# A planned attention and feed-forward kernel: a later due time for the codes of item 23, and pair 19 turned by TensorE

## The chip, the cores and the metric

The kernel runs on one core of one Trainium2 chip. The metric is the device time of one execution in microseconds; the time of a kernel is the median of its runs.

## The reference

There are two stages. In the first, 4 batches of 8 heads with 768 tokens and 64 features attend within clusters: a query sees only the keys that have the same nearest of 16 centroids.

```python
q_assign = np.argmax(np.einsum('bhsd,hcd->bhsc', q_n, c_n), axis=-1)
k_assign = np.argmax(np.einsum('bhsd,hcd->bhsc', k_n, c_n), axis=-1)
mask = q_assign[:, :, :, None] == k_assign[:, :, None, :]
scores = scale * np.matmul(q, k.transpose(0, 1, 3, 2))
scores = np.where(mask, scores, -1000000000.0)
...
attn = np.exp(scores)
attn = attn / (np.sum(attn, axis=-1, keepdims=True) + 1e-09)
return np.matmul(attn, v).astype(np.float32)
```

In the second, the heads of a token are put side by side to a row `x` of 512 values, and 3072 such rows go through a feed-forward layer with 2048 hidden values:

```python
h = x @ w_in
g = h * (1.0 / (1.0 + np.exp(-h)))
return (g @ w_out).astype(np.float32)
```

## The kernel before, in words

**The work.** An *item* `h8` to `h31` is one head of batches 1 to 3, its queries and keys (batch 0 is written out by hand as `plan`). An item's rows are loaded (`load`, line 111), split into two half-precision parts on VectorE (`hi`, line 127, and `lo`, line 132) and turned by a transposing transfer on SP's queue into the tile `ab` (`xpose`, line 141). Then TensorE makes the logits against the centroids (`logits_1`, line 180, 12 small matmuls into `psN`); VectorE sums them, finds the largest and marks it (lines 192, 208, 217). The marks are the item's *codes*: GpSimd scales them (lines 224 and 225), SP turns them (`c_xpose`, line 233, tile `cdt`), and GpSimd's queue moves them into 16 further rows of `ab` (`c_move`, line 237). From then on one matmul over `ab` gives the scores with the mask in them.

**Score units.** There are 192; each is two matmuls of line 356 (`qk_mm`, into one of two `pS` buffers) and one exponential on ScalarE (line 361). Item 23, the last head of batch 2's first half to be reached, is first read by unit 117. When the six units of a pair of heads and one half of the queries are through, 36 matmuls of line 373 (`pv`) multiply with the values, and VectorE normalizes (lines 383 and 385) to the tile `xn`, 128 by 384 values.

**Turned pairs.** Such a *pair* has a number n: n // 8 is the batch, n // 4 % 2 the half of the queries, n % 4 the pair of heads. It must be turned into a quarter of `xt`, the input of the up projection: either by a transposing transfer on SP's queue (`xn_d`, line 414), or by three transposes on TensorE into a PSUM bank `px` (`xn_t`, line 395) and a copy by VectorE or ScalarE (`xn_ev`, lines 406 and 404). `by_dma(n)` chooses.

**Feed-forward.** An up projection (`unit_a`, line 423) is four matmuls, one for each quarter of `xt`, into `ph`; ScalarE and VectorE gate it. The down projections are groups of four matmuls (line 494) or products of eight with sums ahead of them (line 576).

**Order.** There is one queue for each engine and each waits in order. From unit 27 on the order is set by a planner, when the kernel is built: it keeps a clock for each engine, knows for each piece a ready time, a length and a rank, and takes on TensorE what is ready at its clock, the lowest rank first; the other engines take what is ready first. For a score unit the ready time holds `code_at` of its items, which is the planned landing of the codes and a margin (`CODES`, 1.5, for the items of batches 2 and 3). PSUM banks 0 to 3 go around in the order in which the planner has them free. A piece that the planner puts first is waited for on the chip, whether or not something behind it could run.

Of the kernel before, what the change touches and what calls it, by code (L numbers as in the profile page):

```python
# [34 lines left out]
def kernel(  # L35
# [11 lines left out]
    B, H, S, D = q.shape  # L47
# [68 lines left out]
    def hi(job, eng=None, part=None):  # L116
        s = part or slice(0, job.n)
        if job.name not in hls:
            n = len(hls)
            hls[job.name] = mp.tile([128, 12, 2, D], f16, name="hl", tag=f"hl{n % 4 if n < EARLY else n % 3}", bufs=1)  # L120
        o, i = hls[job.name][:, s, 0, :], raws[job.name][:, s, :]
        if eng == "act":
            nc.scalar.activation(out=o, in_=i, func=AF.Copy, bias=0.0, scale=QS)  # L123
        elif eng == "pool":
            nc.gpsimd.tensor_scalar(out=o, in0=i, scalar1=QS, scalar2=None, op0=ALU.mult)
        else:
            nc.vector.tensor_scalar(out=o, in0=i, scalar1=QS, scalar2=None, op0=ALU.mult)

    def lo(job, part=None):
        s = part or slice(0, job.n)  # L130
        hl = hls[job.name]
        nc.vector.scalar_tensor_tensor(  # L132
            out=hl[:, s, 1, :], in0=raws[job.name][:, s, :], scalar=QS, in1=hl[:, s, 0, :], op0=ALU.mult, op1=ALU.subtract
        )

    def xpose(job, part=None):
        s = part or slice(0, job.n)
        hl = hls[job.name]
        if job.name not in abs_:
            abs_[job.name] = mp.tile([128, 12, 128], f16, name="ab", tag=f"ab{place[job.name] % 12}", bufs=1)  # L140
        nc.sync.dma_start_transpose(abs_[job.name][:, s, :], hl[:, s].rearrange("p n c d -> p (n c d)"))
# [44 lines left out]
    def logits_1(job):  # L186
        logits_n(job, None, 2 * HC)

    def lsum(job, last=True):
        g, m, P = job.halves, job.m, Ls[job.name]  # L190
        L = mp.tile([128, 12 * HC], f32, name="L", bufs=2)[:, 0 : g * HC * m].rearrange("p (h c m) -> p h c m", h=g, m=m)
        nc.vector.tensor_reduce(  # L192
            out=L, in_=P.rearrange("p h (n c) m -> p h c m n", n=2), axis=AX.X, op=ALU.add
        )
        if last:
            done(psNs.pop(job.name))
        Ls[job.name] = L
# [7 lines left out]
    def mx_n(job):  # L205
        g, m = job.halves, job.m
        mx = mxn[job.name] = mp.tile([128, 12], f32, name="mxn", bufs=3)
        nc.vector.tensor_reduce(
            out=mx[:, 0 : g * m].rearrange("p (h m) -> p h m", h=g), in_=Ls[job.name].rearrange("p h c m -> p h m c"),
            axis=AX.X, op=ALU.max,  # L210
        )

    def ge_n(job):
        g, m = job.halves, job.m
        nn[job.name] = len(nn)
        mx = mxn.pop(job.name)[:, 0 : g * m].rearrange("p (h m) -> p h m", h=g)
        nc.vector.tensor_tensor(  # L217
            out=ohv(job), in0=Ls.pop(job.name), in1=mx.unsqueeze(2).to_broadcast([128, g, HC, m]), op=ALU.is_ge
        )


    def c_scale(job):
        o = ohv(job)
        nc.gpsimd.tensor_scalar(out=o[:, :, :, 0:3], in0=o[:, :, :, 0:3], scalar1=OHV, scalar2=None, op0=ALU.mult)  # L224
        nc.gpsimd.tensor_scalar(
            out=o[:, :, :, 3:6], in0=o[:, :, :, 3:6], scalar1=OHV, scalar2=-OHV, op0=ALU.mult, op1=ALU.add
        )
# [3 lines left out]
    def c_xpose(job):  # L231
        cd = cds[job.name] = mp.tile([128, 2, 128], f16, name="cdt", tag="cd", bufs=4)
        nc.sync.dma_start_transpose(cd, ohd[nn[job.name] % 3].rearrange("p h n -> p (h n)"))

    def c_move(job):
        cd = cds.pop(job.name)
        nc.gpsimd.dma_start(
            abs_[job.name][64 : 64 + HC, :, :].rearrange("p n c -> p (n c)"), cd[0 : 6 * HC].rearrange("p h c -> p (h c)")
        )

    def cd_mm(job):
        m = (job.n + 1) // 2
        if job.name not in psNs:
            psNs[job.name] = bank("psC")
        for h in range(2):
            nc.tensor.matmul(
                psNs[job.name][0 : m * HC, 256 + 128 * h : 384 + 128 * h], ohv(job)[:, h].rearrange("p c m -> p (c m)"), ident, start=True, stop=True
            )
# [730 lines left out]
    def lands(t, work, rest):  # L979
        nonlocal moves_end  # L980
        moves_end = max(t, moves_end) + work
        return moves_end + rest

    def add(eng, ready, length, f, then=None, late=0.0):
        lanes[eng].append((ready, ready + late, length, f, then))
# [17 lines left out]
    def either(ready, dve, act, f, then=None, late=0.0):  # L1003
        eng = "ACT" if backlog("ACT", ready) + act + MARGIN < backlog("DVE", ready) + dve else "DVE"
        add(eng, ready, act if eng == "ACT" else dve, lambda: f(eng[0]), then, late)
# [6 lines left out]
    code_at, tensor_todo, after_unit, turn_at, after_turn = {}, [], {}, {}, {}  # L1012

    def chain(job, b):
        def split(t):
            old = int(job.name[1:]) - (3 if int(job.name[1:]) >= H + 8 else 4)
            if old >= H + 2 and old not in turn_at:
                after_turn[old] = split
                return
            if job.name not in loaded:  # L1020
                waiting[job.name] = split
                return
            t = max(t, loaded[job.name] + 0.4, turn_at.get(old, 0.0) + 0.3)
            either(t, 0.5, 0.72, lambda e: hi(job, "act" if e == "A" else None), lambda t: add("DVE", t, 0.9, lambda: lo(job), turned, 1.5), 1.5)

        def turned(t):
            i = int(job.name[1:])
            split_at.setdefault(i, t)
            if i in after_split:
                after_split.pop(i)(t)  # L1030
            u = last_use.get(place[job.name] - 12, 0)
            if u not in read_at:
                after_unit.setdefault(u, []).append(lambda x: turned(max(t, x)))
                return
            t = max(t, read_at[u] + 0.06)
            add("SP", t, lambda t: min(max(1.7, moves_end - t), 8.0), lambda: xpose(job), lambda t: landed(lands(t, 1.49, 1.41)), 0.0 if b == 1 else 3.0)

        def landed(t):
            i = int(job.name[1:])
            turn_at[i] = t  # L1040
            t_start(t)
            if i in after_turn:
                after_turn.pop(i)(t)
            turning(t + ROOM[b - 1])

        def turning(t):
            tensor_todo.append((t, 0.35, lambda: logits_1(job), sums))

        def sums(t):
            add("DVE", t + 0.2, 0.52, lambda: lsum(job), lambda t: add("DVE", t, 0.47, lambda: mx_n(job), top, 0.6), 0.6)  # L1050

        def top(t):
            add("DVE", t, 0.33, lambda: ge_n(job), codes, 0.6)

        def codes(t):
            if job.late:
                add("POOL", t, 1.05, lambda: c_scale(job), lambda t: add("SP", t, 1.3, lambda: c_xpose(job), moved))
            else:
                tensor_todo.append((t + 0.06, 0.11, lambda: cd_mm(job), out_of_bank))

        def moved(t):
            add("POOL", lands(t, 0.71, 1.4) + 0.1, 0.58, lambda: c_move(job), lambda t: known(t, 0.52, 0.87, CODES))

        def out_of_bank(t):
            either(t + 0.2, 0.44, 0.44, lambda e: cd_ev(job, e), lambda t: by_sync(t), 0.3)

        def by_sync(t):
            clock["SP"] = max(clock["SP"], t) + 0.65
            known(clock["SP"], 0.63, 0.98, 1.0)

        def known(t, work, rest, room):
            code_at[job.name] = lands(t, work, rest) + room

        return split

# [63 lines left out]
    for i in range(H, B * H):  # L1139
        b, h = divmod(i, H)  # L1140
        p = SPLIT[i - H]
        job = jobs[i]
# [58 lines left out]
    def t_start(t):  # L1201
        ready_t[0] += 1
        if ready_t[0] == B * H - H + 1 and any(n > 1 for x in QUADS.values() for n in x):
            t_step(0, t, 1)
# [20 lines left out]
    work = {hb: 16 * 0.655 + sum(3.452 if x in (0, 1, 2) else 6.118 for x in kinds[hb]) for hb in kinds}  # L1225
# [2 lines left out]
    unit = FIRST  # L1228

    def by_dma(n):  # L1230
        return 8 <= n < 8 * B - 1 and n != 11

    def norm_piece(n, t):
        b, c, i = n // 8, n // 4 % 2, n // 8 * H + 2 * (n % 4)
# [381 lines left out]
    while True:  # L1616
# [11 lines left out]
        t, e, piece = best  # L1628
# [34 lines left out]
```

## Time and profile before

| what | us |
|---|---|
| median of 3 runs (lowest, highest) | 298.42 (297.69, 299.86) |
| the profiled execution | 297.59 |
| its span, first to last instruction | 295.8 |
| busy: TensorE, VectorE, ScalarE, GpSimd | 286.2, 234.8, 228.5, 72.0 |

The profile is of one execution, 0.83 us under the median of the three runs. PE is TensorE's matmuls, PEld its weight loads, DVE VectorE, ACT ScalarE, POOL GpSimd, SP the queue that issues most transfers; a q behind an engine's name is its queue of instructions that only issue. A row's L number is a line of the kernel.

### The profile page before, as it was taken

Reading aid. Unit: us, or ns where it says so; the run is one execution under the profiler, and the core shown is the slowest. Engines: PE = TensorE matmul, PEld = TensorE weight load, DVE = VectorE, ACT = ScalarE, POOL = GpSimd, SP = SyncE. Lnnn points to the kernel's source line nnn. Section 1 sums busy time; section 2 is a strip of 40 time slices with the busy share of each in tenths; the row PEclk is TensorE's granted clock in tenths of the full one; section 3 lists DMA queues with packets and bytes.
Section 4 is the critical chain, followed back from the end, with each engine's and each line's share of the span. In section 5 each row is a group of like instructions: output and inputs, shape, how many; then the busy total and the mean of one; then the engine's idle time right before and its main releaser. Section 6 shows DMA issues by size and latency. Waiting matters only on the chain.

```text
span 295.8 us, 8471 instructions
## 1 busy us (share of the span) xinstructions
PE 286.2 (97%) x3369; PEld 209.2 (71%) x3369; DVE 234.8 (79%) x517; ACT 228.5 (77%) x385; POOL 72.0 (24%) x130
## 2 busy tenths in 40 slices
PE   7999989999999999999999899999999999999995
PEld 3777746566766566668766775768787878888984
DVE  5999688486897799997797845989868788778862
ACT  5999789755996579988588577997889987967621
POOL 5485610001041015653232471224210000000000
PEclk9999999999999999999999999999999999999999
DMA  6869999998966499999947969896130011110013
GB/s 208 268 170 198 231 217 194 120 296 175 252 147 166 123 193 271 226 192 228 215 137 149 199 165 259 185 150 133 32 99 17 13 51 51 49 39 2 11 63 142
DMA packets 78710, 44.63 MB, mean 151 GB/s; under 512 B 56240, under 2 KB 75600, under 8 KB 78672
## 3 DMA queue, kind: packets, MB, share of 16 engines
q1 hardware_dynamic: 71840, 35.50, 53.7%
q0 software_dynamic: 6288, 8.13, 14.3%
q8 instruction: 26, 0.43, 0.6%
q10 hardware_dynamic: 544, 0.48, 0.5%
q14 instruction: 12, 0.10, 0.1%
HBM read 27.30 MB, written 6.29 MB: 114 GB/s over the span
## 4 chain that ended last, share of the span: by engine, by line
PE 80%; DMA 13%; ACT 3%; issue 1%; DVE 1%; SPq 0%; POOL 0%; ACTq 0%; DVEq 0%
PE ph L423 19%; PE pS L356 17%; PE po L576 15%; PE pO L373 9%; PE po L494 8%; PE ph L717 5%; DMA win_s<-in_moe_w_in_dram 4%; PE psN L180 3%; DMA ab<-hl 2%; DMA vn<-in_v_dram 2%; DMA xt<-xn 2%; PE py L717 2%; DMA ab<-cdt 1%; DMA ab<-cd 1%; ACT P L361 1%
## 5 line engine op out<-in xcount | busy, mean ns | idle before, releaser
L361 ACT ACTIVATE P<-pS 128x768 f16<-128x768 f32 x192 | 156.2, 824 | 35.7 <-PE pS L356 34.8
L356 PE MATMUL pS<-ab 128*128 128x384 f16 x384 | 93.3, 326 | 1.5 <-DMA ab<-cdt 0.8
L423 PE MATMUL ph<-xt,win_s 128*128 128x384 f16 x384 | 75.5, 326 | 1.7 <-DMA win_s<-in_moe_w_in_dram 1.4
L451 DVE SCALAR_TENSOR_TENSOR gt<-tn,ph 128x384 f16<-128x384 f32 x90 | 48.3, 549 | 13.7 <-ACT tn L448 12.7
L423 PEld LDWEIGHTS <-win_s 128*128 128x128 f16 x384 | 36.5, 98 | 24.0 <-DMA win_s<-in_moe_w_in_dram 1.8
L448 ACT ACTIVATE tn<-ph 128x384 f32<-128x384 f32 x90 | 45.1, 512 | 3.8 <-PE ph L423 3.3
L356 PEld LDWEIGHTS <-ab 128*128 128x128 f16 x384 | 34.1, 98 | 19.5 <-issue 1.3
L373 PEld LDWEIGHTS <-P 128*128 128x128 f16 x1152 | 39.8, 97 | 3.7
L373 PE MATMUL pO<-vt,P 128*128 128x65 f16 x1152 | 41.4, 193 | 0.0
L297 POOL CAST vt<-vn 128x384 f16<-128x384 f32 x32 | 19.3, 612 | 58.9 <-DMA vn<-in_v_dram 56.2
L494 PE MATMUL po<-wout_s,gt 128*128 128x512 f16 x128 | 32.5, 379 | 0.6 <-DMA wout_s<-in_moe_w_out_dram 0.6
L132 DVE SCALAR_TENSOR_TENSOR hl<-raw,hl 128x768 f16<-128x768 f32 (+3 forms) x39 | 31.5, 821 | 0.6 <-ACT hl L123 0.3
L576 PEld LDWEIGHTS <-gt 128*128 128x128 f16 x272 | 26.3, 98 | 4.8
L224 POOL TENSOR_SCALAR od<-od 128x96 f16<-128x96 f16 x16 | 10.3, 642 | 55.3 <-DVE od L217 55.3
L576 PE MATMUL po<-wout_s,gt 128*128 128x256 f16 x176 | 22.8, 273 | 0.0
L494 PEld LDWEIGHTS <-gt 128*128 128x128 f16 x128 | 12.0, 98 | 11.4 <-issue 0.8
L180 PEld LDWEIGHTS <-ab 128*128 128x128 f16 x458 | 17.0, 97 | 3.5 <-DMA ab<-hl 0.4
L385 DVE TENSOR_TENSOR xn<-pO,zr 128x384 f16<-128x384 f32 x32 | 17.8, 557 | 1.1
L180 PE MATMUL psN<-stk,ab 128*128 128x32 f16 (+1 forms) x458 | 18.3, 188 | 0.1
L576 PE MATMUL po<-tw,sg 128*128 128x256 f16 x144 | 18.3, 273 | 0.0
L192 DVE TENSOR_REDUCE L<-psN 128x192 f32<-128x384 f32 (+1 forms) x27 | 14.8, 549 | 3.4 <-PE psN L180 3.3
L576 PEld LDWEIGHTS <-sg 128*128 128x128 f16 x160 | 15.5, 98 | 2.3
(130 smaller groups left out, 345.5 us busy)
## 6 DMA issues: line engine op xcount, KB each, us to landing
raw<-in_k_dram SPq DMA_DIRECT2D x31, 192.0 KB, 3.9
out_dram<-ot SPq DMA_DIRECT2D x23, 256.0 KB, 2.3
raw<-in_q_dram SPq DMA_DIRECT2D x24, 192.0 KB, 3.9
vn<-in_v_dram SPq DMA_DIRECT2D x16, 192.0 KB, 4.5
vn<-in_v_dram POOLq DMA_DIRECT2D x16, 192.0 KB, 4.0
wout_s<-in_moe_w_out_dram POOLq DMA_DIRECT2D x4, 512.0 KB, 19.4
win_s<-in_moe_w_in_dram POOLq DMA_DIRECT2D x3, 512.0 KB, 10.5
raw<-in_q_dram SPq DMA_DIRECT2D x2, 384.0 KB, 4.1
```

Source lines behind the costliest of these rows:

```text
L132: nc.vector.scalar_tensor_tensor(out=hl[:, s, 1, :], in0=raws[job.name][:, s, :], scalar=QS, in1=hl[:, s, 0, :], op0=ALU.mult, op1=ALU.sub ...
L180: nc.tensor.matmul(L[:, n % g, :, n // g], ab[:, i, :], stk[:, job.groups[i // 3][0], x : x + w], start=(x == 0), stop=(x + w == 2 * HC),)
L297: nc.gpsimd.tensor_copy(vt[:, :, 0:D], vns.pop(i))
L356: nc.tensor.matmul(pS[:, e, 0:HALF], abs_[kj.name][:, kn, :], rhs, start=True, stop=True)
L361: nc.scalar.activation(out=P, in_=pst.pop(u)[:, :, 0:HALF], func=AF.Exp, bias=0.0, scale=ESC)
L373: nc.tensor.matmul(o[:, (2 * t + h) * VW : (2 * t + h + 1) * VW], Ps[i + h, c, j // 2][:, j % 2, ts(t, 128)], vtb[(i + h) % 13][:, j, 0:VW ...
L423: nc.tensor.matmul(ph[:, 0:HALF], win_s[:, r, ts(fb, 128)], xts[b, c][:, r, :], start=(r == 0), stop=(r == NR - 1))
L448: nc.scalar.activation(out=tn, in_=ph[:, 0:HALF], func=AF.Tanh, bias=0.0, scale=1.0)
L451: nc.vector.scalar_tensor_tensor(out=gt[:, fb, :], in0=tn, scalar=1.0, in1=ph[:, 0:HALF], op0=ALU.add, op1=ALU.mult)
L494: nc.tensor.matmul(po, gts[b, c][:, fc, ts(t, 128)], wout_s[:, fc, :], start=(fc == 0), stop=(fc == NFB - 1))
L576: nc.tensor.matmul(o, l[:, f, :], x, start=(f == 0 and k in begins), stop=(f == HK - 1), skip_group_check=True)
L717: nc.tensor.matmul(o[:, HT * j : HT * j + HT], w, x, start=(k in (1, 2, 5, 3) and j == 0 and r == 0), stop=(r == 1), skip_group_check=True,)
```

## The change

Two numbers of the planner's input are altered. The codes of item 23 get 0.8 more behind their planned landing before the planner takes them as known, and pair 19 (batch 2, first half of the queries, last two heads: the last quarter that the up projections of that half need) is turned by TensorE in place of a transposing transfer.

```diff
         def known(t, work, rest, room):
-            code_at[job.name] = lands(t, work, rest) + room
+            code_at[job.name] = lands(t, work, rest) + room + (0.8 if job.name == "h23" else 0.0)
...
     def by_dma(n):
-        return 8 <= n < 8 * B - 1 and n != 11
+        return 8 <= n < 8 * B - 1 and n not in (11, 19)
```

Everything ahead of unit 117 on TensorE is as before. On TensorE, unit 117 stands before behind a product of batch 1; `ab_3062` is the tile of item 23's keys, `ab_3382` that of item 26:

```order
L576 MATMUL po2_3514<-wout_s_67,gt_3077 128x256
L356 LDWEIGHTS ab_3062
L356 MATMUL pS_3526<-ab_3062 128x384
L356 LDWEIGHTS ab_3062
L356 MATMUL pS_3526<-ab_3062 128x384
L180 LDWEIGHTS ab_3382
L180 MATMUL psN_3530<-stk_68,ab_3382 128x32
```

Now the twelve logits matmuls of item 26 follow that product, and these rows are their end:

```order
L180 LDWEIGHTS ab_3382
L180 MATMUL psN_3526<-stk_68,ab_3382 128x32
L356 LDWEIGHTS ab_3062
L356 MATMUL pS_3540<-ab_3062 128x384
L356 LDWEIGHTS ab_3062
L356 MATMUL pS_3540<-ab_3062 128x384
L576 LDWEIGHTS sg_3443
L576 MATMUL po_3491<-tw_2216,sg_3443 128x256
```

So the logits of item 26 and the score unit 117 have changed places; the next product (`sg`) comes after both, as before. Six score units later, still on TensorE, pair 19 (`xn_3660`) is turned between unit 123 and the product behind it:

```order
L356 LDWEIGHTS ab_2293
L356 MATMUL pS_3678<-ab_2293 128x384
L395 LDWEIGHTS xn_3660
L395 MATMUL px_3682<-ident_84,xn_3660 128x128
L395 LDWEIGHTS xn_3660
L395 MATMUL px_3682<-ident_84,xn_3660 128x128
L395 LDWEIGHTS xn_3660
L395 MATMUL px_3682<-ident_84,xn_3660 128x128
L576 LDWEIGHTS gt_3077
L576 MATMUL po_3491<-tw_2318,gt_3077 128x256
```

The six rows of line 395 are new; VectorE's copy of `px` stands behind both passes over item 27. On SP's queue, the first row here ends the load of item 29, a minus is a row of before and a plus one of the change (`xt<-xn` is a pair, `ab<-hl` an item, here first 27 and then 28, `out_dram<-ot` results):

```order
 L111 DMA raw<-in_k_dram 128x384
-L414 DMA_TRANSPOSE xt<-xn 128x3x128
+L141 DMA_TRANSPOSE ab<-hl 128x12x128
 L611 DMA out_dram<-ot 128x2x256
-L141 DMA_TRANSPOSE ab<-hl 128x12x128
-L506 DMA out_dram<-ot 128x512
 L111 DMA raw<-in_q_dram 128x384
 L111 DMA raw<-in_k_dram 128x384
+L506 DMA out_dram<-ot 128x512
+L141 DMA_TRANSPOSE ab<-hl 128x12x128
```

Pair 19 has gone from there, and the turns of items 27 and 28 stand further ahead. With them the logits of items 27 and 28 move on TensorE, each ahead of two up projections that it followed; on GpSimd the scaling of item 27's codes comes ahead of two casts of values. Further on, near unit 153, two products of batch 2 change places with an up projection each, and from unit 159 on TensorE's order is that of before.

## The prediction

> **What bounds the kernel now.** I read the page's busy shares first, then the table of windows, and last the timeline of TensorE (PE) at the two windows in which it isn't full. In the first row stand busy microseconds and share of the span for each engine, in the second PE's busy tenths in 40 slices of 7.4 us; the window rows give the busy time of PE, weight loads, VectorE, ScalarE and GpSimd in 5 us, then the granted clock, the DMA share and GB/s.
>
> ```profile
> PE 286.2 (97%) x3369; PEld 209.2 (71%) x3369; DVE 234.8 (79%) x517; ACT 228.5 (77%) x385; POOL 72.0 (24%) x130
> ...
> PE   7999989999999999999999899999999999999995
> ...
> 165.00:170.00 5.00, 4.25 (x46) 3.27 (x44) 4.00 (x9) 2.89 (x5) 1.95 (x5) 1.00 1.10 258
> ...
> 180.00:185.00 5.00, 4.72 (x45) 2.93 (x42) 2.15 (x5) 4.17 (x8) 0.00 (x0) 1.00 0.92 271
> ```
>
> PE is busy for 97% of the span, so a change here can win only what PE waits, and every piece added to PE is paid in full unless a wait swallows it. In the stretch that the change touches PE loses 0.75 us in the window from 165 and 0.28 in the one from 180. The clock stays at 1.00 through both, so nothing but order, waits and added pieces counts. The slices are all nines from the one after 170 us to the next to last: a shift that PE has by 185 us reaches the end, since no later wait takes it up.
>
> The first wait, on PE and on its weight loads (start, length, what; the bracket has the idle time and what ended it):
>
> ```profile
> 165.86 1.04 PE L576 MATMUL po<-wout_s,gt 128*128 128x256 f16 x8
> 167.65 0.50 PE L356 MATMUL pS<-ab 128*128 128x384 f16 x2 [0.75 <-DMA ab<-cdt]
> 167.98 0.51 PE L180 MATMUL psN<-stk,ab 128*128 128x32 f16 x12
> 168.33 1.04 PE L576 MATMUL po<-tw,sg 128*128 128x256 f16 x8
> 169.21 0.49 PE L356 MATMUL pS<-ab 128*128 128x384 f16 x2
> ...
> 167.64 0.11 PEld L356 LDWEIGHTS <-ab 128*128 128x128 f16 x2 [1.03 <-DMA ab<-cdt]
> 167.94 0.44 PEld L180 LDWEIGHTS <-ab 128*128 128x128 f16 x12 [0.18 <-DMA ab<-hl]
> ```
>
> A row's end includes the pipeline's drain, so I take distances between starts: 8 matmuls of a product cost 169.21 - 168.33 = 0.88, 12 of a logits group 168.33 - 167.98 = 0.35, the two of a score unit 0.33. The product that began at 165.86 was issued by 166.74, and PE then stood 0.91 us for item 23's codes. The last row is the one to see: when the scores had gone, the logits of item 26 found **their own data barely there**, as their weight load too was ended by a transfer.
>
> How long both transfers had been under way (the chain's row for item 23's codes, then the transposing transfer of item 26 and its time from issue to landing):
>
> ```profile
> 163.28 4.33 DMA ab<-cdt
> ...
> L141 SPq DMA_TRANSPOSE ab<-hl x1: 1458/1458/1458, 162.4 to 162.4; - x1
> DMA to landing us min/median/max: 5.5/5.5/5.5
> ```
>
> The codes landed at 163.28 + 4.33 = 167.61, item 26's rows at about 162.4 + 5.5 = 167.9, which the weight load at 167.94 confirms.
>
> **Part 1, the margin.** In the new order the logits of item 26 stand ahead of the score unit. SP's queue and the moves on GpSimd that issue those two transfers are in the same order as before, so I leave both landings where they are. Then PE waits, after 166.74, not until 167.65 but until 167.98; the logits run from 167.98 to 168.33 as they did, and only then come the scores, 0.33, which had run inside that wait. The next product starts at 168.66 in place of 168.33: **+0.33 us**. Were item 26's rows there before 166.74, the logits would fill 0.35 of the wait and the product would start at 167.98: -0.35. These are the two ends; the row at 167.94 decides for the first. The exponential of this unit also moves 0.68 later, but the next score unit that needs its buffer is two further on, at 169.21 + 0.33 + 0.88 = 170.4, and an exponential lasts 0.824:
>
> ```profile
> L361 ACT ACTIVATE P<-pS 128x768 f16<-128x768 f32 x192 | 156.2, 824 | 35.7 <-PE pS L356 34.8
> ```
>
> From about 168.9 it is done by 169.8: no second wait.
>
> **Part 2, the pair on TensorE.** What three such turns cost on PE shows where the kernel does them already:
>
> ```profile
> 108.26 0.33 PE L395 MATMUL px<-ident,xn 128*128 128x128 f16 x3
> 108.43 0.49 PE L356 MATMUL pS<-ab 128*128 128x384 f16 x2
> ...
> L395 PE MATMUL px<-ident,xn x30: 217/219/230, 29.1 to 262.6; 128*128 128x128 f16 x30
> L406 DVE COPY xt<-px x8: 345/357/359, 31.2 to 73.7; 128x384 f16<-128x384 f16 x8
> ```
>
> From start to start the three take 108.43 - 108.26 = **+0.17 us**; a single one lasts 0.219 but they overlap. The Trainium skill speaks against such a move: "TensorE: Matmul & The Clock Gate", Part 4: PE-mode transpose, gives about 275 ns for one 128x128 turn inside a kernel and adds that its output goes to PSUM and needs a copy. By that, three one after the other would be an estimated 0.83 us; the rows here show 0.17, a fifth of it, and the measurement decides.
>
> The copy of 0.357 lands on VectorE behind the two passes over item 27, whose rows are these, with PE's and the SP queue's of the same time:
>
> ```profile
> 174.64 0.56 DVE L385 TENSOR_TENSOR xn<-pO,zr 128x384 f16<-128x384 f32 x1
> 175.70 1.20 DVE L132 SCALAR_TENSOR_TENSOR hl<-raw,hl 128x768 f16<-128x768 f32 x1
> 176.82 0.68 DVE L609 TENSOR_TENSOR ot<-po,uu 128x512 f32<-128x512 f32 x1
> 180.60 0.20 DVE L383 RECIPROCAL zr<-pO 128x6 f32<-128x6 f32 x1 [0.73 <-PE pO L373]
> ...
> 175.41 0.49 PE L356 MATMUL pS<-ab 128*128 128x384 f16 x2
> 175.73 0.49 PE L576 MATMUL po<-tw,gt 128*128 128x256 f16 x3
> ...
> 178.22 3.08 SPq L141 DMA_TRANSPOSE ab<-hl  x1
> ```
>
> With the +0.33 of part 1 the normalized pair is ready at 174.64 + 0.56 + 0.33 = 175.53, and PE reaches the turn, which stands between the two PE rows, at 175.73 + 0.33 = 176.06: no wait, with 0.5 to spare. VectorE is through item 27 at 175.70 + 1.20 + 0.33 = 177.23 and has the copy at 177.6, four microseconds before it is used. What stands behind it there starts 0.36 later; the idle 0.73 ahead of the normalization at 180.60 covers that, and if it didn't, a PSUM bank would come free up to 0.36 later.
>
> The wait that goes, and the chain's row for its transfer:
>
> ```profile
> 180.73 0.65 PE L423 MATMUL ph<-xt,win_s 128*128 128x384 f16 x3
> 181.66 0.32 PE L423 MATMUL ph<-xt,win_s 128*128 128x384 f16 x1 [0.28 <-DMA xt<-xn]
> 182.14 0.81 PE L423 MATMUL ph<-xt,win_s 128*128 128x384 f16 x4
> 182.79 0.49 PE L356 MATMUL pS<-ab 128*128 128x384 f16 x2
> ...
> 176.32 5.30 DMA xt<-xn
> ```
>
> Four such matmuls take 182.79 - 182.14 = 0.65, so the fourth was due at 180.73 + 0.49 = 181.22 and came at 181.66: **-0.44 us** of real standing still (the 0.28 counts from the modelled end). The sum is +0.33 + 0.17 - 0.44 = **+0.06 us**. In other words, PE gets there 0.50 late, at 181.72, when even the old transfer (landed at 176.32 + 5.30 = 181.62) would have been in time. Each edit's worth hangs on the other: the margin alone would be swallowed whole by the second wait, and the turn then removes only 0.11 of wait for its 0.17.
>
> **Part 3, what moves along.** SP loses the transposing issue that stood at 176.32, so item 27's turn goes out as soon as VectorE is through, at 177.23 in place of 178.22 (the row above), and that one took 5.5:
>
> ```profile
> L141 SPq DMA_TRANSPOSE ab<-hl x1: 3076/3076/3076, 178.2 to 178.2; - x1
> DMA to landing us min/median/max: 5.5/5.5/5.5
> ```
>
> Its logits also move two up projections ahead on PE:
>
> ```profile
> 183.77 0.49 PE L356 MATMUL pS<-ab 128*128 128x384 f16 x2
> ...
> 186.04 0.51 PE L180 MATMUL psN<-stk,ab 128*128 128x32 f16 x12
> ...
> DMA to landing us min/median/max: 3.7/5.0/6.4
> ```
>
> They will stand behind the scores of 183.77, that is at 183.77 + 0.33 + 0.06 = 184.16, instead of 186.04. Behind them on PE waits everything. The last row is for all transposes of items from 100 us on: with the slowest, 6.4, the data are there at 183.6, with the old one's 5.5 at 182.7. No wait, 0.5 us to spare at least. The later swap near 210, two products of the batch-2 pair ahead of two up projections, needs a VectorE sum of before for the second product's operand:
>
> ```profile
> 213.10 0.41 DVE L602 TENSOR_TENSOR ot<-po,uu 128x256 f32<-128x256 f32 x1
> 215.06 1.04 PE L576 MATMUL po<-wout_s,gt 128*128 128x256 f16 x8
> ```
>
> The sum ends at 213.51, and that product moves from 215.06 up by one piece (0.98 less the 0.06) to about 214.1. Cost: nothing, with 0.6 to spare. On GpSimd the scaling of item 27's codes, which waits for VectorE until about 187, now stands ahead of two casts of values, and so these start some 10 us late; the product that first reads them on PE comes behind that of 215.06, so nothing waits. From there on PE's order is the old one.
>
> **The rivals.** (a) *The logits fill the wait.* If in most executions item 26's rows land before 166.74, part 1 is -0.35, PE reaches the second place early, and the sum is -0.35 + 0.17 - 0.44 = -0.62. For it speaks the median of 5.0 above against 5.5 here; against it, that 4.3 would be needed. (b) *Slower: the second wait was this execution's own.* The page has for these transfers a median of 3.0:
>
> ```profile
> xt<-xn SPq DMA_TRANSPOSE x22, 3.0
> ```
>
> From a landing of 181.22 - 176.32 = 4.9 or less there is no wait to remove; then +0.33 + 0.17 = +0.50 stays. For it: 3.0; against it: the next transposing transfer, of 178.2, took 5.5 as well, so that stretch of the queue was full, not one transfer unlucky. (c) *The three turns don't overlap*: 3 x 0.219 = 0.66, that is 0.49 more than counted, +0.55 in all. The rows at 108 us speak against it. The Trainium skill's figure in Part 4, quoted above, would have it so. (d) *Slower by over 1%: item 27's logits come too early.* They wait when the landing takes over 184.16 - 177.23 = 6.9. While the weights load, the same transfer took a median of 12.1:
>
> ```profile
> DMA to landing us min/median/max: 6.7/12.1/15.4
> ```
>
> That would cost 5.2 us; nothing so heavy is in flight at 177 us.
>
> **How the numbers follow.** The profiled execution took 297.59 in a span of 295.8, the three runs a median of 298.42, that is 0.83 above it. Forecast: 297.65 by the execution, 298.5 by the median; chance 0.57. (a) 297.8, 0.20. (b) 298.9, 0.15. (c) 299.0, 0.04. (d) 303.6, 0.04. A measurement of this kernel can tell about 1% from no change, 3 us; only (d) is past it. The three runs reached from 0.73 below their median to 1.44 above, so I take half a microsecond to 0.7 around the outer cases (a) and (c): 297.2 to 299.7. Faster by over 1% 0.02, within 0.94, slower 0.04.
>
> **What would show it.** Right: a wait of about 1.1 ahead of the *logits* near 167.9, ended by the transfer of item 26's rows, none ahead of the scores; no wait at the fourth matmul near 181.7; 33 turning matmuls in place of 30; PE's busy time up by 0.1 to 0.2. Wrong: a wait under 0.5 near 167 (a), or any wait ahead of the logits near 184 (d).

## The result and the profile after

The changed kernel takes 299.74 us (median of 14 runs) against 298.27 of the kernel before in 14 runs beside them: a ratio of 1.0058, with a 95% interval from 1.003 to 1.0086. That is 1.7 us more, 0.9 to 2.6 by the interval, where +0.06 was forecast; the median lies just above the range of 297.2 to 299.7. The ratio and its interval, here and in the experiments, leave out slow executions (over 1.5% above the fastest of their kernel), so it is not quite the quotient of the medians. The profiled execution took 299.67 in a span of 297.8.

The page of the changed kernel, busy shares and PE's slices:

```profile
PE 287.7 (97%) x3372; PEld 209.8 (70%) x3372; DVE 235.6 (79%) x518; ACT 228.0 (77%) x385; POOL 70.7 (24%) x130
...
PE   7899999999999999999999999999899999999995
```

The 8 that stood at 163 to 170 us has gone, and there is one in the slice from 208 to 216, where before was a 9. So PE's timeline in the changed kernel at the two places of the prediction, and at the new one:

```profile
166.57 1.04 PE L576 MATMUL po<-wout_s,gt 128*128 128x256 f16 x8
167.65 0.52 PE L180 MATMUL psN<-stk,ab 128*128 128x32 f16 x12
168.63 0.50 PE L356 MATMUL pS<-ab 128*128 128x384 f16 x2 [0.46 <-DMA ab<-cdt]
168.97 1.04 PE L576 MATMUL po<-tw,sg 128*128 128x256 f16 x8
...
176.37 0.33 PE L395 MATMUL px<-ident,xn 128*128 128x128 f16 x3
176.53 0.82 PE L576 MATMUL po<-tw,gt 128*128 128x256 f16 x6
...
181.53 0.81 PE L423 MATMUL ph<-xt,win_s 128*128 128x384 f16 x4
182.18 0.49 PE L356 MATMUL pS<-ab 128*128 128x384 f16 x2
...
209.50 0.65 PE L423 MATMUL ph<-xt,win_s 128*128 128x384 f16 x3
211.09 0.32 PE L423 MATMUL ph<-xt,win_s 128*128 128x384 f16 x1 [0.94 <-DMA xt<-xn]
```

The product that starts at 166.57 is issued by 166.57 + 0.88 = 167.45. In this execution the logits of item 26 start 0.20 later, and most of the wait stands behind them, 0.63 of the scores for the codes (from 167.65 + 0.35 = 168.00 to 168.63): the other way around than I forecast. The three turning matmuls take 176.53 - 176.37 = 0.16, and the four matmuls at 181.53 go through in 182.18 - 181.53 = 0.65, without a wait: both as forecast. The last two rows are new. The first up projection of batch 2's second half has three quarters of its input, and its fourth matmul, due at 209.50 + 0.49 = 209.99, comes at 211.09: 1.10 us of standing still for a pair's transposing transfer, that of pair 23. The kernel before has no wait there at all.

### The profile page after: what moved, and what is told of

The parts are those of the page before. It is cut to its first block, busy times and chain, and to the rows that moved or that the text cites. A ratio compares the mean times of both kernels' runs of the same rounds, so it can differ in the third digit from the quotient of the medians.

```text
span 297.8 us, 8474 instructions
## 1 busy us (share of the span) xinstructions
PE 287.7 (97%) x3372; PEld 209.8 (70%) x3372; DVE 235.6 (79%) x518; ACT 228.0 (77%) x385; POOL 70.7 (24%) x130
## 5 line engine op out<-in xcount | busy, mean ns | idle before, releaser
L297 POOL CAST vt<-vn 128x384 f16<-128x384 f32 x32 | 18.3, 581 | 62.3 <-DMA vn<-in_v_dram 54.2
L132 DVE SCALAR_TENSOR_TENSOR hl<-raw,hl 128x768 f16<-128x768 f32 (+3 forms) x39 | 32.2, 837 | 0.8 <-ACT hl L123 0.5
L224 POOL TENSOR_SCALAR od<-od 128x96 f16<-128x96 f16 x16 | 9.6, 597 | 49.4 <-DVE od L217 49.3
```

Of the source, the lines that this page charges most:

```text
L132: nc.vector.scalar_tensor_tensor(out=hl[:, s, 1, :], in0=raws[job.name][:, s, :], scalar=QS, in1=hl[:, s, 0, :], op0=ALU.mult, op1=ALU.sub ...
L297: nc.gpsimd.tensor_copy(vt[:, :, 0:D], vns.pop(i))
```

## Where pair 23 was held up

SP's queue in the changed kernel (start, time to issue, what), with the time that pair 23's transfer then took to land:

```profile
202.03 1.17 SPq L233 DMA_TRANSPOSE cdt<-od  x1
203.29 1.45 SPq L141 DMA_TRANSPOSE ab<-hl  x1
204.84 0.87 SPq L539 DMA_DIRECT2D cp<-gt  x1
205.81 2.40 SPq L414 DMA_TRANSPOSE xt<-xn  x1
...
DMA to landing us min/median/max: 5.2/5.2/5.2
```

The same issues in the kernel before; that of item 29's codes ends just ahead of the first row:

```profile
201.49 1.43 SPq L141 DMA_TRANSPOSE ab<-hl  x1
203.04 0.84 SPq L539 DMA_DIRECT2D cp<-gt  x1
203.97 1.60 SPq L414 DMA_TRANSPOSE xt<-xn  x1
...
DMA to landing us min/median/max: 3.8/3.8/3.8
```

All that stands behind item 29's codes on the queue is 1.8 us late: the turn of item 31 at 203.29 against 201.49, pair 23 at 205.81 against 203.97. It lands at 205.81 + 5.25 = 211.05 (5.2 in the row is rounded) against 203.97 + 3.8 = 207.8. Item 29's codes must be scaled by GpSimd ahead of their turn, and here is GpSimd in the changed kernel:

```profile
200.36 0.54 POOL L237 DMA_DIRECT2D ab<-cdt  x1 [5.07 <-PE pS L356]
200.92 0.84 POOL L224 TENSOR_SCALAR od<-od 128x96 f16<-128x96 f16 x1
201.71 0.29 POOL L225 TENSOR_SCALAR od<-od 128x96 f16<-128x96 f16 x1
```

And in the kernel before:

```profile
199.23 0.73 POOL L224 TENSOR_SCALAR od<-od 128x96 f16<-128x96 f16 x1 [2.06 <-DVE od L217]
199.90 0.30 POOL L225 TENSOR_SCALAR od<-od 128x96 f16<-128x96 f16 x1
...
201.38 0.59 POOL L237 DMA_DIRECT2D ab<-cdt  x1
```

Before, GpSimd scaled item 29's codes (lines 224 and 225) as soon as VectorE had them, and moved item 28's (line 237) later. In the changed order the move of item 28's codes stands first. It has to wait until their turn has landed, GpSimd idles for 5.07 us ahead of it, and the scaling behind it starts at 200.92 instead of 199.23. Of these 1.69 us about 0.5 are not the swap's, since VectorE itself had item 29's codes only at 199.27 + 0.35 = 199.62 in this execution, against 199.15 before:

```profile
199.27 0.35 DVE L217 TENSOR_TENSOR od<-L,mxn 128x192 f16<-128x192 f32 x1
```

So a move of which nothing is needed for long holds a scaling, the scaling holds SP's queue, and the queue holds pair 23. (The row names a score unit as what ended the wait, since it came last; the turn of item 28's codes had landed 0.66 before, as the last section shows.)

VectorE pays at the same place. Its order has the first sum over the pair's tile ahead of a normalization now, and it idles until the transfer lands:

```profile
211.17 0.36 DVE L657 TENSOR_TENSOR xs<-xt 128x384 f16<-128x384 f16 x1 [2.42 <-DMA xt<-xn]
```

## The experiments

From here *theory Q* is the chain above: GpSimd's swap makes SP's queue late and PE waits near 210. In the diffs, line 1062 is where a landed turn of codes is handed to GpSimd for its move. Each kernel was timed in 12 runs, with runs of the kernel before on the same chip.

**The margin alone.**

```diff
-            code_at[job.name] = lands(t, work, rest) + room
+            code_at[job.name] = lands(t, work, rest) + room + (0.8 if job.name == "h23" else 0.0)
```

> Only the margin behind item 23's codes; pair 19 stays a transposing transfer. The order differs from before by one swap on TensorE (logits of item 26 ahead of score unit 117) and one on GpSimd. Theory Q (the queue: the time is lost because GpSimd's move of item 28's codes stands ahead of the scaling of item 29's, so that SP's queue issues the turn of pair 23 late, and the first up projection of batch 2's second half waits): nothing of that is in this kernel, so no wait near 210, and the same time as before within 0.4 us. Theory M (the margin's swap is what costs, by more than the 0.33 forecast): slower than before by about 1.7 us, with waits over 1.5 us in all near 167.

Measured 297.03 against 297.02 us, a ratio of 1.000 (0.997 to 1.003): theory M falls. PE near the swap, near the old second wait, and near 210:

```profile
165.46 1.04 PE L576 MATMUL po<-wout_s,gt 128*128 128x256 f16 x8
167.28 0.52 PE L180 MATMUL psN<-stk,ab 128*128 128x32 f16 x12 [0.79 <-DMA ab<-hl]
167.64 0.49 PE L356 MATMUL pS<-ab 128*128 128x384 f16 x2
167.96 1.04 PE L576 MATMUL po<-tw,sg 128*128 128x256 f16 x8
...
180.36 0.81 PE L423 MATMUL ph<-xt,win_s 128*128 128x384 f16 x4
...
208.18 0.81 PE L423 MATMUL ph<-xt,win_s 128*128 128x384 f16 x4
```

In this execution it goes, at the swap, as I had forecast for the whole change: the logits wait for their own data, the scores behind them for nothing. The wait at the fourth matmul of the first up projection is not there even though pair 19 still comes by transfer; PE is not late there either, 180.36 against 180.73 before.

**The turn of pair 19 alone.**

```diff
-        return 8 <= n < 8 * B - 1 and n != 11
+        return 8 <= n < 8 * B - 1 and n not in (11, 19)
```

> Only pair 19 on TensorE, without the margin; all of the order near 190 to 212 is that of the change. Theory Q: as slow as the change, 0.8 to 1.8 us over before, with a wait of about 1 us for a pair's transposing transfer near 210. Theory M: no slower than before, -0.3 to +0.2 us.

Measured 299.17 against 297.02 us, 1.0068 (1.0039 to 1.0096): the turn alone is as slow as both edits together. Its profile has the late chain, but not the wait. First GpSimd, then SP, then PE:

```profile
201.38 0.54 POOL L237 DMA_DIRECT2D ab<-cdt  x1 [4.87 <-PE ph L423]
201.94 1.04 POOL L224 TENSOR_SCALAR od<-od 128x96 f16<-128x96 f16 x1
...
207.01 2.25 SPq L414 DMA_TRANSPOSE xt<-xn  x1
...
210.72 0.84 PE L423 MATMUL ph<-xt,win_s 128*128 128x384 f16 x4
...
PE psN L180 <- DMA ab<-hl: 2.4, 3, 1.4
PE pS L356 <- DMA ab<-cdt: 1.3, 1, 1.3
```

The move stands ahead of the scaling again and pair 23 goes out at 207.01, but PE reaches the up projection at 210.72, over a microsecond later than in the changed kernel, having lost 2.4 and 1.3 us in waits that the last two rows show. These lie from 128 to 152 us, in the part of the order that is the same in all these kernels. Pair 23's transfer took 4.2 in this execution and landed at 207.01 + 4.2 = 211.2, just when the late PE came to its fourth matmul, 210.72 + 0.49 = 211.21. So this one execution doesn't show the wait that I expected of it, and the verdict on the turn rests on its time and on the runs that follow.

**Both edits, and the move of item 28's codes later.**

```diff
-            add("POOL", lands(t, 0.71, 1.4) + 0.1, 0.58, lambda: c_move(job), ...
+            add("POOL", lands(t, 0.71, 1.4) + 0.1 + (2.0 if job.name == "h28" else 0.0), 0.58, lambda: c_move(job), ...
```

> The change whole, but GpSimd's move of item 28's codes is planned 2 us later, which alters one thing in the whole order: it stands behind the scaling of item 29's codes instead of ahead of it. Theory Q: the turn of pair 23 is issued near 204 instead of 205.8, the wait near 210 goes or falls under 0.3 us, and the time is that of before, -0.6 to +0.3 us. Theory L (the load on the transfer queues, or VectorE's new order, makes the turn late whatever GpSimd does): the wait near 210 stays at about 1 us and the time is 0.8 to 1.8 us over before.

Measured 297.36 against 297.02 us, 1.0016 (0.998 to 1.0052): same as before. GpSimd, SP and PE:

```profile
198.72 0.71 POOL L224 TENSOR_SCALAR od<-od 128x96 f16<-128x96 f16 x1 [4.43 <-DVE od L217]
199.59 0.57 POOL L237 DMA_DIRECT2D ab<-cdt  x1
...
203.46 1.53 SPq L414 DMA_TRANSPOSE xt<-xn  x1
...
208.50 0.81 PE L423 MATMUL ph<-xt,win_s 128*128 128x384 f16 x4
209.15 0.49 PE L356 MATMUL pS<-ab 128*128 128x384 f16 x2
```

With that one instruction behind the scaling, pair 23 goes out at 203.46, its transfer is in time and the four matmuls take 0.65. Theory L falls as far as it says that the wait stays whatever GpSimd does. A part of it remains: the transfer took 5.3 here too and landed at 208.7, only 0.2 to 0.3 ahead of the fourth matmul (208.50 + 0.49 = 208.99); before it took 3.8 and had a slack of 1.7. In this execution, then, most of the slack is used up even without the swap on GpSimd; why the transfer takes longer is not shown. Nor do the times of this run and of the change lie clear of each other, 0.998 to 1.0052 against 1.003 to 1.0086.

**The kernel before, and the move of item 28's codes earlier.** The same line with -3.0 in place of 2.0, in the kernel before, without either edit.

> The kernel before, with neither edit, and one thing altered in its order: GpSimd's move of item 28's codes stands ahead of the scaling of item 29's and of a cast. Theory Q: the turn of pair 23 is issued 1 to 2 us later than before's 203.97, the first up projection of batch 2's second half waits 0.4 to 1.5 us near 210, and the time is 0.4 to 1.5 us over before. Theory M and theory L: nothing, within 0.2 us of before.

Measured 298.8 against 297.02 us, 1.0046 (1.0017 to 1.0076): the swap alone makes the old kernel slower. GpSimd, SP and PE:

```profile
202.18 0.57 POOL L237 DMA_DIRECT2D ab<-cdt  x1 [3.92 <-PE pS L356]
202.78 0.49 POOL L224 TENSOR_SCALAR od<-od 128x96 f16<-128x96 f16 x1
...
207.30 1.57 SPq L414 DMA_TRANSPOSE xt<-xn  x1
...
210.08 0.65 PE L423 MATMUL ph<-xt,win_s 128*128 128x384 f16 x3
211.91 0.32 PE L423 MATMUL ph<-xt,win_s 128*128 128x384 f16 x1 [1.17 <-DMA xt<-xn]
```

The chain and the wait are there without a single transpose more on PE: 211.91 - 210.08 - 0.49 = 1.34 us at the fourth matmul. Pair 23 goes out 3.33 later than before, more than the 1 to 2 expected, but 1.09 of that PE had lost earlier (210.08 against 208.99 before), in waits of 1.3 and 0.8 between 128 and 152 us, where the order is that of before. This run and the one above move the same one instruction in opposite directions, and the wait follows.

**The turn alone, and the move later.** The edit of the second run with that of the third.

> The turn of pair 19 by TensorE without the margin, and GpSimd's move of item 28's codes planned 2 us later, so that it stands behind the scaling of item 29's codes. It differs from the run with the turn alone by that one swap on GpSimd. Theory Q (the swap makes SP's queue late and the up projection near 210 wait): the 0.68% of the turn alone goes, the time is -0.6 to +0.3 us against before, no wait over 0.3 us near 210. Theory S (the turn itself costs, by its transposes, the PSUM bank and VectorE's copy): 0.8 us or more over before remain, whatever GpSimd does.

Measured 297.99 against 297.72 us, 0.9997 (0.9959 to 1.0035). The 0.68% of the turn has gone, and here the two intervals are clear of each other (1.0039 to 1.0096 with the turn alone), so theory S falls: three transposes, a bank and a copy of 0.36 cost nothing that can be measured. PE at the first place and near 210:

```profile
167.99 0.50 PE L356 MATMUL pS<-ab 128*128 128x384 f16 x2 [1.10 <-DMA ab<-cdt]
...
209.07 0.81 PE L423 MATMUL ph<-xt,win_s 128*128 128x384 f16 x4
```

**Both edits with a margin of 2.0.**

```diff
-            code_at[job.name] = lands(t, work, rest) + room
+            code_at[job.name] = lands(t, work, rest) + room + (2.0 if job.name == "h23" else 0.0)
```

> The change with a margin of 2.0 in place of 0.8: score unit 117 then stands behind the logits of item 26 and two more products, and the order on GpSimd has the scaling of item 29's codes ahead of the move of item 28's by itself; much of the order up to unit 159 differs from both kernels. Theory Q: no wait near 167, none over 0.3 near 210; -1.2 to 0.0 us against before. Theory S: 0.8 us or more over before.

Measured 298.47 against 297.72 us, 1.0034 (0.9999 to 1.007): not the gain that theory Q allowed. Its middle, +1.0 us, lies where theory S had put it, though theory S falls by the run above. The wait near 167, which was to go, is still there:

```profile
168.52 0.52 PE L180 MATMUL psN<-stk,ab 128*128 128x32 f16 x12 [1.29 <-DMA ab<-hl]
```

More margin moves the scores, but the logits of item 26 still stand first and wait for their own transfer, here for 1.29. Much of the order is new in this kernel, so it decides nothing on theory Q, and where the rest of its time goes stays open.

None of these is measurably faster than the kernel before.

## Why the prediction was wrong

*What bounds it* held as far as the profiles show it: the clock stayed at 1.00, and the loss that was found is a wait of PE. The sign "PE's busy time up by 0.1 to 0.2" did not come: it went from 286.2 to 287.7. It can't tell so little, as the run with the move early has 287.0 without a piece added to PE.

*Part 1, the margin* (+0.33, bounds -0.35 and +0.33): both ways of waiting occur. The logits wait for their data in the run with the margin alone and in that with 2.0; in the changed kernel and in the run with the move later, the scores do most of the waiting. Which of two transfers lands last differs from one execution to the next, so rival (a) had as good a right as the forecast. Neither bound came in size. From the product ahead of the swap to the product behind it PE took 168.97 - 166.57 = 2.40 in the changed kernel and 167.96 - 165.46 = 2.50 with the margin alone. Before it was 168.33 - 165.86 = 2.47, and 2.80 was forecast. These executions show no cost of the swap, and the time of the margin alone, 1.000 within 0.3%, could not tell the two bounds apart.

*Part 2, the turn on TensorE* (+0.17, -0.44): the 0.16 was measured, and there is no wait at 181.7. But that wait was not the turn's to win. The run with the margin alone does not have it, and neither does the run with the move early, which has the order of before up to GpSimd's swap near 200 and turns pair 19 by a transfer. Here is PE in that run, at the first place and at the up projection:

```profile
168.32 1.04 PE L576 MATMUL po<-wout_s,gt 128*128 128x256 f16 x8
...
169.87 1.04 PE L576 MATMUL po<-tw,sg 128*128 128x256 f16 x8
...
182.27 0.81 PE L423 MATMUL ph<-xt,win_s 128*128 128x384 f16 x4
```

The four matmuls go through, as rival (b) said: the wait of 0.44 is in none of these profiles but the one that the forecast was read from. Nor is the first wait there. From product to product it is 169.87 - 168.32 = 1.55, no more than the pieces take (0.88 + 0.33 + 0.35 = 1.56); PE had already waited 2.1 us between 128 and 152 in this execution. So both prices, +0.33 and -0.44, were read from one execution and hold for it alone. That each edit's worth hangs on the other is not shown, since PE was not late at the up projection with the margin alone. Rival (c) falls with the 0.16, and with it the estimate from the Trainium skill's "TensorE: Matmul & The Clock Gate", Part 4: PE-mode transpose. Its 275 ns is for one transpose inside a kernel, and here three of them overlap.

*Part 3, what moves along*, is **the step that failed**, with its sentence on GpSimd: "the scaling of item 27's codes [...] now stands ahead of two casts of values [...] so nothing waits". I had read that swap and taken the casts for all that moved. A little further on in the same queue the move of item 28's codes had passed the scaling of item 29's. I followed neither what that move waits for, nor that SP's queue stands behind the scaling, nor what is last in that queue: the last quarter of the next up projections' input. I asked of the pieces near 210 only whether VectorE had their sums ready, not whether pair 23's transfer was. In the kernel before its slack could be read. It landed at 207.8, and the matmuls that read it are these:

```profile
208.99 0.81 PE L423 MATMUL ph<-xt,win_s 128*128 128x384 f16 x4
```

The fourth came at 208.99 + 0.49 = 209.48, so the slack was 1.7 us. The issue came 1.84 later and the transfer took 1.4 more; less the 1.7 and the 0.5 that PE itself was later in this execution, about 1.1 is left, which is the wait.

The term missing from the sum is that wait: by the changed kernel's execution +1.10, by the reversed experiment +1.34 in a kernel without either edit. It lies inside the measured 0.9 to 2.6. That the whole 1.7 is this wait is not shown to a tenth, as one profile is one execution. That it is the bulk, the two runs with the move late indicate. Their middles are 0.16% above before and 0.03% below it, and by the upper ends of their intervals they lie within 0.5% and 0.4% of it. By time alone two comparisons are clear of noise, the turn with and without the late move, and the kernel before with and without the early one. In the profiles the wait is there with the swap and gone without it, but for the run with the turn alone.

Rival (d), item 27's logits waiting for their data, did not come about; no row of these profiles shows that wait.

## What to carry to other kernels

When a schedule is replanned, go through each in-order queue and look for a waiting instruction that has moved ahead of one which is ready; then follow the ready one to the next queue that stands behind it, and to the end of that queue. Price it by slack: the landing of the last transfer of that queue against its first reader, both read from the old trace. And before a wait is taken for a price, read the same place in a second profile of the same order. An edit that removes a wait of half a microsecond can start a chain like this in an engine that is busy for a quarter of the time.

## What the runs showed of the hardware

GpSimd took 0.66 us from a landing to the issue that waits for it. The turn of item 28's codes was issued at 194.81 in the changed kernel and landed after this time:

```profile
194.81 1.19 SPq L233 DMA_TRANSPOSE cdt<-od  x1
...
DMA to landing us min/median/max: 4.9/4.9/4.9
```

That is 199.7, and the move starts at 200.36, 0.66 later. In the run with the turn alone the same turn was issued at 196.02 and took 4.7, and the move starts at 201.38, again 0.66 later. The second surprise is how much one program's executions differ in their waits: in the profile of the turn alone PE lost 3.7 us from 128 to 152, in that of the move early 2.1, in that of the changed kernel 0.6, and in that of the kernel before nothing there, with the same order on all queues up to then. In the first two PE then had no wait near 167.
